# A prologue in a new order, stack loads in halves and last sums on three engines, in a fused attention and gMLP block

## The chip, the cores and the metric

The kernel runs on one core of one Trainium2 chip. The metric is device time of one execution in microseconds; shown are the median of three runs and one execution taken by the hardware profiler. The core has five engines that run side by side and wait for each other by semaphores: PE (TensorE, matrix products; PEld is its weight load), DVE (VectorE), ACT (ScalarE), POOL (GpSimd) and SP (SyncE, which here only issues DMAs). DMAs move data between the chip's main memory and the on-chip memory.

## What is computed

A transformer block with two parallel branches on one sequence of S = 2048 tokens of width D = 512, 32 heads of 16, and a hidden width of 1792, split in two halves of 896:

```python
xn = layernorm(x)
q, k, v = split_heads(xn @ wqkv)                 # 32 heads of 16
o = softmax(q @ k.T / 4) @ v                     # per head, 2048 x 2048 scores
attention = merge(o) @ wo
z = gelu(xn @ w_in)
z1, z2 = z[:, :896], layernorm(z[:, 896:])
g = w_sp @ z2 + b_sp[:, None]                    # mixes over the tokens
mlp = (z1 * g) @ w_out
out = x + attention + mlp
```

All is float32. Where a product needs more than the matmul's own precision, an operand is written as the sum of two parts ("split" into high and low), and three products are added.

## The kernel before

**One program in two pieces.** The instruction streams of all engines are written out in order by the kernel itself; nothing reorders them afterwards. The first piece, the *prologue*, is a list of words, `STEPS`, which the class `First` turns into instructions one word at a time, so the place of a word fixes the place of its instructions on every engine that it uses. The second piece comes from a *planner* in the kernel's host code: it keeps a planned clock for each engine, asks at each step what TensorE may do next and emits it.

**Words of the list.** The four groups g of 512 tokens are written as the first digit:

- S: statistics of two token tiles on VectorE (bn_stats, L1006); R: their reciprocal root; N: the normalisation on GpSimd (L1023), with a star the second tile on ACT.
- T: four transposes on TensorE (L1028) into a PSUM tile; E: copy of the result to SBUF, split, by ACT and VectorE (L244).
- Q g a: the projection to q (a = 0) or k (a = 1) of the first eight heads, 12 matmuls (L247 to L249). F g a: its eviction, split and store to main memory (`qscr`, `kscr`; two DMAs). Without a star ACT makes the high part and VectorE the low part (L244); with one ACT copies twice and GpSimd subtracts (L1058).
- L g: the load of the first head pair's q and k *stacks* for that token group back into SBUF (`qst`, `kst`; four DMAs of 96 KB). M kc t: a product of q tile t and k group kc (L1100, TensorE), for which the stacks must have landed; X kc t: its row maximum on VectorE (L1105).
- VH, VL: the split of the weight of v (a star: on GpSimd, L1076 and L1082); V, VE: the first tiles of v. WH, WL, B: split of the weights of q and k and of the bias. Z g c: a 512 KB store of the transposed tokens to `xscr`, by SP. The other twelve such stores (tokens of groups 1 to 3) are issued by GpSimd behind the list (`keep`, L1142).

A PSUM tile is taken in turn out of four, so a T, Q, V or M also waits until the tile's last reader is through.

**DMAs.** `move` (L142) issues on SP, in the order of the program. SP uses eight completion semaphores in turn, so each DMA waits until the one eight before it has landed.

**The planner.** The attention runs over 16 head pairs p, four groups of 512 queries c and 16 key tiles kt. TensorE's stream is made of *scores* (S, L1212), *maxima* of the pair to come (M, L1226; the maximum is L823 on VectorE), *value groups* (V, L1313: 32 matmuls on eight exponentials; 128 of them, V1 to V128) and *dense* slots (D, L1271), which take the rest of the block's products from a queue: rest of v, rest of q and k, z2, z1, the mixing over tokens (`spatial`, with pieces `zs0` to `zs111` of z2 and the split weight `wsp`), the gMLP's output product and at last the attention's output product (`attn_out`). A slot is two matmuls of 512 columns on the two halves of the array. `ORDER` is the pattern between two value groups. Where nothing else may be issued, the planner emits a *filler* slot (L1285), a product with zeros.

`LOADZ` is the planned time from the issue of a `zs` piece to its landing; the planner lets no dense slot that uses it stand earlier than that by its clock. `hold` (L1252) stops the queue at a unit's end in a gap between two value groups once more than eight dense slots have been placed in it.

**Stacks.** `load_stacks` (L802) loads the q and k stacks of pair p + 1 while pair p runs: four DMAs of 384 KB, spaced 2.7 us apart in the planner's clock (`later`, unit `HALF`).

**The end.** The last pair's heads go through `last_pair` (L943, sums of the softmax), `last_norm` (L955, reciprocal and product on VectorE), `last_mm` (L964, product with `wo`, by way of a selection) and `last_add` (L971), which adds the product to `fin`, the finished rest of two token tiles (t = 0, 2, ... 14), and stores it. `last_turn` decides when a `last_mm` may come. Tasks have a priority; a lower number goes first.

Of the kernel before, what the change touches and what calls it, by code (L numbers as in the profile page):

```python
# [16 lines left out]
P = 128  # L17
# [29 lines left out]
PF = 8  # L47
WARM = 22
STEPS = (
# [5 lines left out]
)  # L55
CYC = 8
FINE = 24
LOAD = 5.0
LOADZ = 5.0
HALF = 2.7  # L60
SLOT = 0.23
TURN = 0.2
# [6 lines left out]
def fused_block(ctx, tc, x, wqkv, wo, w_in, w_spT, b_sp, w_out, out):  # L69
# [18 lines left out]
    def ta(n):  # L88
        return 0.2 + n / 1220.0
# [51 lines left out]
    def move(dst, src):  # L141
        nc.sync.dma_start(raw(dst), raw(src))  # L142
# [13 lines left out]
    def later(k, fn, *args):  # L156
        at(clock() + k * HALF, fn, *args)
# [34 lines left out]
    def spawn(gen, prio=2, ready=None):  # L192
        count[0] += 1
        ends[0] = clock() if ready is None else ready
        queue_up(gen, prio, count[0], ends[0])
# [606 lines left out]
    def load_stacks(p, cols=slice(0, S)):  # L802
        m, r = p // 4, (p % 4) * 2
        q, k = qst[p % 2], kst[p % 2]
        sl = [slice((r + j) * DH, (r + j + 1) * DH) for j in range(2)]
        for j in range(2):
            for i, (t, scr) in enumerate(((q, qscr), (k, kscr))):
                args = t[64 * j:64 * j + KS, cols], scr[m][sl[j], :, cols]
                if p and 2 * j + i:
                    later(2 * j + i, move, *args)  # L810
                else:
                    move(*args)

    NSTEP = NP * 64
    mmax = {}
# [127 lines left out]
    def last_pair(c, e, k):  # L943

        ones = sel["ones"]
        two = piece(f"on{c}").bitcast(F32)
        rec, on = two[:, 0, 0:P], two[:, 1, 0:P]
        acc = sl[k][:, 1, :]
        for b in (1, 0):
            for u in range(4):  # L950
                nc.tensor.matmul(acc[32 * u:32 * u + 32, b * P:(b + 1) * P], ones[:, 0, 32 * b:32 * b + 32], e[:, u * P:(u + 1) * P], start=True, stop=True)
        T["P"] += 0.5
        spawn(last_norm(c, acc, rec, on, k), 0, T["P"] + 0.2)

    def last_norm(c, acc, rec, on, k):  # L955
        yield "D", 0.95
        nc.vector.reciprocal(rec, acc[:, P:2 * P])  # L957
        yield "D", 0.3
        nc.vector.tensor_mul(on, acc[:, 0:P], rec)
        free_slot(k)  # L960
        for i in range(2):
            turn.append((c, on, ends[0] + 0.1, i))
# [6 lines left out]
        spawn(last_add(4 * c + 2 * i, k), 0, T["P"] + 0.2)  # L969

    def last_add(t, k):  # L971
        yield "D", 1.22
        nc.vector.tensor_add(fin[t], sl[k], fin[t])
        free_slot(k)
        for a in range(2):
            after(0.1, move, out[(t + a) * P:(t + a + 1) * P, :], fin[t][:, a, :])

# [136 lines left out]
    with tc.manual_schedule(engines=engines):  # L1114
# [64 lines left out]
        def free_slot(k):  # L1179
            pending[k] -= 1  # L1180
            if not pending[k]:
                slotfree[k], kind[k] = ends[0] + 0.08, ""
# [54 lines left out]
        def has_dense(t):  # L1237
            nonlocal blocked, swap, hold, seen
            while not slots:
                if blocked > t or dfree[0] > t or hold or not queue:  # L1240
                    return False
                it = next(queue[0], None)
                if it is None:
                    queue.pop(0)
                elif it[0] == "t":
                    slots.extend(it[1])
                elif it[0] == "w":
                    blocked = t + it[1]
                elif it[0] == "s":
                    swap = True  # L1250
                elif it[0] == "q":
                    hold = spent > 8 and n_pv < N and len(vdone) == NT - EARLY  # L1252
                elif it[0] == "e":
                    dfree[0] = FAR
                    held[0] = len(it[1])
                    for g in it[1]:
                        spawn(g, 0, T["P"] + 0.25)
            if swap and seen < lastd:
                nc.tensor.drain()
                seen = pe  # L1260
                T["P"] += DRAIN
            swap = False
            return True
# [81 lines left out]
        def spare(t):  # L1345
            return [k for k in range(3) if slotfree[k] <= t]

        def last_turn(t):
            c, on, when, i = turn[0]
            if when > t or added.get(4 * c + 2 * i, FAR) + 0.1 > t or len(spare(t)) < 2:  # L1350
                return False
            turn_to("L")
            last_mm(c, on, i, take("l"))
            turn.pop(0)
            return True
# [77 lines left out]
```

## Time and profile before

| | |
|---|---|
| median of three runs | 1849.95 us (1849.7 to 1851.14) |
| profiled execution, its own time | 1848.92 us |
| its span in the profile | 1847.1 us |
| TensorE busy | 1809.0 us |
| VectorE busy | 1445.7 us |
| ScalarE busy | 1210.1 us |
| GpSimd busy | 673.9 us |
| row maxima on VectorE (L823) | 1008 of 1222 ns |
| exponentials on ScalarE (L86) | 1024 of 1026 ns |

In timelines a row is: start, length, engine, line, operation, destination and source, count, and in brackets the engine's idle time just before it and what ended it. In the chain of waits a row is start, length, and the engine or transfer that the end hung on. Windows give each engine's busy time in a stretch, the granted clock of TensorE as a share of full speed, the busy share of the DMA engines and their rate.

### The profile page before, as it was taken

To read this page: it belongs to the slowest core of one execution; us is meant where nothing else is said; L and a number is where in the kernel's file an instruction comes from. 1 tells how busy PE (TensorE), PEld (TensorE's weight loads), DVE (VectorE), ACT (ScalarE), POOL (GpSimd) and SP (SyncE) were. 2 spreads that over 40 slices of the span, in tenths; PEclk is the share of its full clock that TensorE was granted. 3 is DMA by queue.
4 is the path that set the end of the run, shared out by engine and by line. 5 is a ranking of instruction groups with operands and counts; after the bars stand their busy time and mean duration, and the time that the engine had idled before them with its cause. 6 is when DMAs were issued, how large, how long until landed. Compare 5 with 4: busy or idle time off the path is not lost.

```text
span 1847.1 us, 38060 instructions
## 1 busy us (share of the span) xinstructions
PE 1809.0 (98%) x14774; PEld 1094.1 (59%) x14774; DVE 1445.7 (78%) x1700; ACT 1210.1 (66%) x1329; POOL 673.9 (36%) x778
## 2 busy tenths in 40 slices
PE   8999999999999999999999999999999999999998
PEld 6655656656656656566665655656556566665543
DVE  7857887888887877778877887778778878787883
ACT  4247777888877777666666665666656666565665
POOL 3442142677758677112532244103422240002200
PEclk9999999999999999999999999999999999999999
DMA  7666754434664337657857567665767566575422
GB/s 273 236 235 197 218 193 147 122 110 121 162 201 118 123 82 217 151 150 180 220 160 202 155 193 186 163 148 158 181 170 183 178 177 141 143 185 141 128 86 81
DMA packets 211069, 305.63 MB, mean 165 GB/s; under 512 B 36784, under 2 KB 106992, under 8 KB 208000
## 3 DMA queue, kind: packets, MB, share of 16 engines
q1 hardware_dynamic: 203400, 275.93, 53.8%
q0 software_dynamic: 7488, 27.27, 4.3%
q8 instruction: 116, 1.90, 0.4%
q14 instruction: 65, 0.53, 0.1%
HBM read 193.27 MB, written 109.85 MB: 164 GB/s over the span
## 4 chain that ended last, share of the span: by engine, by line
PE 87%; DVE 5%; DMA 3%; POOL 1%; issue 1%; SPq 1%; ACT 1%; DVEq 0%; POOLq 0%; ACTq 0%
PE dps L1271 35%; PE sl L1313 23%; PE sl L1212 14%; PE sl L1226 12%; DVE mm L823 4%; SPq L142 1%; PE dps L1285 1%; DMA zs<-z2scr 1%; POOL wsp L288 1%; PE sl L247 1%; PE sl L249 0%; PE sl L248 0%; ACT pf L86 0%; DMA wsp_10r<-in_w_spT 0%; PE sl L967 0%
## 5 line engine op out<-in xcount | busy, mean ns | idle before, releaser
L823 DVE TENSOR_REDUCE mm<-sl 128x2 f32<-128x1024 f32 x1008 | 1208.0, 1222 | 200.5 <-PE sl L1226 193.0
L86 ACT ACTIVATE pf<-sl 128x1024 f32<-128x1024 f32 x1024 | 1042.5, 1026 | 327.4 <-PE sl L1212 288.5
L1313 PE MATMUL sl<-pf,vall 128*32 128x512 f32 x4096 | 467.9, 595 | 0.7 <-DVE on L957 0.6
L1212 PE MATMUL sl<-qst,kst 50*128 50x512 f32 x2048 | 434.8, 418 | 8.4 <-DVE mm L823 2.5
L1226 PE MATMUL sl<-kst,qst 48*128 48x512 f32 x2016 | 414.9, 404 | 4.5 <-DVE mm L823 2.9
L1271 PE MATMUL dps<-wsp,zs 64*128 64x512 f32 x2352 | 380.3, 393 | 2.2 <-DMA zs<-z2scr 1.8
L1212 PEld LDWEIGHTS sl<-qst,kst 50*128 50x128 f32 x2048 | 194.5, 184 | 220.8 <-issue 82.1
L1313 PEld LDWEIGHTS sl<-pf,vall 128*32 128x32 f32 x4096 | 119.3, 109 | 266.6 <-issue 234.6
L1226 PEld LDWEIGHTS sl<-kst,qst 48*128 48x128 f32 x2016 | 192.3, 185 | 101.9 <-ACT pf L86 49.5
L1271 PEld LDWEIGHTS dps<-wsp,zs 64*128 64x128 f32 x2352 | 227.5, 187 | 40.7 <-DMA zs<-z2scr 2.5
L86 ACT ACTIVATE e<-sl 128x512 f32<-128x512 f32 x64 | 38.3, 598 | 199.5 <-PE sl L1313 188.5
L1335 DVE TENSOR_TENSOR e<-sl,e 128x512 f32<-128x512 f32 x64 | 44.3, 692 | 119.3 <-PE sl L1313 53.6
L729 POOL TENSOR_TENSOR hhl<-z1i,hhl 128x512 fp32r<-128x512 f32 x28 | 36.0, 1292 | 271.7 <-ACT hhl L86 271.7
L1271 PE MATMUL dps<-w,xt 64*128 64x448 f32 x768 | 110.4, 368 | 1.7
L1271 PE MATMUL dps<-wout,hp 64*128 64x512 f32 x672 | 109.9, 392 | 0.0
L874 POOL TENSOR_TENSOR ob<-ob 128x512 f32<-128x512 f32 (+1 forms) x16 | 20.5, 1281 | 198.2 <-DMA ob<-rscr 181.5
L1271 PEld LDWEIGHTS dps<-w,xt 64*128 64x128 f32 x768 | 73.4, 186 | 16.4 <-issue 8.5
L1271 PEld LDWEIGHTS dps<-wout,hp 64*128 64x128 f32 x672 | 65.1, 187 | 9.4
L397 POOL TENSOR_TENSOR qkhl<-qr,qkhl 128x512 fp32r<-128x512 f32 x24 | 30.4, 1283 | 102.0 <-ACT qkhl L86 79.0
L1271 PE MATMUL dps<-wf,zs 64*128 64x512 f32 x336 | 55.3, 392 | 0.1
L870 POOL TENSOR_TENSOR ob<-ob 128x512 f32<-128x512 f32 (+1 forms) x16 | 20.9, 1306 | 93.2 <-DMA ob<-escr 90.9
L1271 PE MATMUL dps<-xnT,wqk 64*128 64x512 f32 x288 | 48.1, 394 | 0.3
(290 smaller groups left out, 1699.2 us busy)
## 6 DMA issues: line engine op xcount, KB each, us to landing
zs<-z2scr SPq DMA_DIRECT2D x192, 256.0 KB
escr<-e SPq DMA_DIRECT2D x60, 256.0 KB
hscr<-hhl POOLq DMA_DIRECT2D x28, 512.0 KB, 6.6
qst<-qscr SPq DMA_DIRECT2D x30, 384.0 KB
kst<-kscr SPq DMA_DIRECT2D x30, 384.0 KB
qscr<-qkhl SPq DMA_DIRECT2D x16, 512.0 KB
kscr<-qkhl SPq DMA_DIRECT2D x16, 512.0 KB
xt<-xscr SPq DMA_DIRECT2D x64, 128.0 KB
```

What stands on the lines that cost most here:

```text
L86: return nc.scalar.activation(out, in_, func, **kw)
L142: nc.sync.dma_start(raw(dst), raw(src))
L397: nc.gpsimd.tensor_sub(hl[:, 1, :], raw_, hl[:, 0, :].bitcast(F32))
L729: nc.gpsimd.tensor_sub(hl[:, 1, :], z1, hl[:, 0, :].bitcast(F32))
L823: nc.vector.tensor_reduce(mmax[g][:, :, t, kc], sl[k], AX.X, ALU.max)
L870: nc.gpsimd.tensor_add(both_[rows, 0, :], both_[rows, 0, :], both_[rows, 1, :])
L874: nc.gpsimd.tensor_mul(both_[rows, 0, :], both_[rows, 0, :], both_[rows, 1, :])
L1212: nc.tensor.matmul(sl[k][:, j, :], kst[p % 2][rows, kt * P:(kt + 1) * P], qst[p % 2][rows, c * 512:(c + 1) * 512], start=True, stop=True)
L1226: nc.tensor.matmul(sl[k][:, j, :], qst[p % 2][rows, tt * P:(tt + 1) * P], kst[p % 2][rows, kc * 512:(kc + 1) * 512], start=True, stop=True)
L1271: nc.tensor.matmul(dps[:, bank, :w], lhs, rhs, start=go, stop=stop)
L1313: nc.tensor.matmul(sl[k][cols:cols + VW, 0, :], vpack(kt + r, 2 * p + j), pf[:, j * 512:(j + 1) * 512], start=n % CYC == 0, stop=n % CYC = ...
L1335: nc.vector.tensor_add(e, sl[k][:, 0, :], e)
```

## The change

Six edits in one:

- `STEPS` is another list. The number of words of each kind is the same. The four Z words stand at its end. Z stores were on SP in the middle. One F more has a star (three instead of two), three VL instead of one, and two N instead of five; most other words stand in another order.
- `LOADZ` goes from 5.0 to 6.5.
- `load_stacks` of pairs from the second on is cut in two halves of the columns: eight DMAs of 192 KB, each half a unit after the one before.
- `last_norm` has priority -1 instead of 0.
- `last_add` of t = 8 and 10 copies the product to SBUF on ACT and adds on GpSimd (planned 2.6 us).
- `hold` depends on there being maxima left (`n_mx < NSTEP`), and `last_turn` needs one free PSUM tile instead of two once the values are done.

```diff
 STEPS = (
-    "S00 S01 R00 WH0 N00 WL0 R01 S10 N01* T01 S11 WH1 T03 E03 T00 E01 R10 T02 WL1 E02 E00 R11 N10 N11* Q00 T13 T12 "
...
-    "X01 M23 VE3 X22 V0 VE0 X12 M21 X23 M20 X21 L3 M11 V1 X20 M32 M30 X11 M31 X32 X31 VE1 V2 X30 M33 X33 VE2 "
+    "S00 S01 R00 WH0 N00 WL0 R01 N01 S10 S11 T01 T02 WH1 R10 E01 R11 T00 N11 T03 E02 WL1 N10 E00 VH2* E03 S21 VH3* "
...
+    "VE0 M20 L3 M23 X20 M22 X23 X22 V1 M33 M31 VE1 X33 M32 V2 M30 X32 X31 X30 VE2 Z00 Z01 Z02 Z03 "
 )
-LOADZ = 5.0
+LOADZ = 6.5
...
-        for j in range(2):
-            for i, (t, scr) in enumerate(((q, qscr), (k, kscr))):
-                args = t[64 * j:64 * j + KS, cols], scr[m][sl[j], :, cols]
-                if p and 2 * j + i:
-                    later(2 * j + i, move, *args)
-                else:
-                    move(*args)
+        n = 0
+        for part in (slice(0, S // 2), slice(S // 2, S)) if p else (cols,):
+            for j in range(2):
+                for t, scr in ((q, qscr), (k, kscr)):
+                    args = t[64 * j:64 * j + KS, part], scr[m][sl[j], :, part]
+                    if n:
+                        later(n / 2, move, *args)
+                    else:
+                        move(*args)
+                    n += p > 0
...
-        spawn(last_norm(c, acc, rec, on, k), 0, T["P"] + 0.2)
+        spawn(last_norm(c, acc, rec, on, k), -1, T["P"] + 0.2)
...
     def last_add(t, k):
-        yield "D", 1.22
-        nc.vector.tensor_add(fin[t], sl[k], fin[t])
-        free_slot(k)
+        if t // 4 == 2:
+            copy = piece(f"last{t}").bitcast(F32)
+            yield "A", ta(1024)
+            act(copy, sl[k], AF.Copy)
+            free_slot(k)
+            yield "G", 2.6
+            nc.gpsimd.tensor_add(fin[t], copy, fin[t])
+        else:
+            yield "D", 1.22
+            nc.vector.tensor_add(fin[t], sl[k], fin[t])
+            free_slot(k)
...
-                    hold = spent > 8 and n_pv < N and len(vdone) == NT - EARLY
+                    hold = spent > 8 and n_mx < NSTEP and len(vdone) == NT - EARLY
...
-            if when > t or added.get(4 * c + 2 * i, FAR) + 0.1 > t or len(spare(t)) < 2:
+            if when > t or added.get(4 * c + 2 * i, FAR) + 0.1 > t or len(spare(t)) < 1 + (n_pv < N):
```

What moves in the engines' order is shown at three places.

The first is SP's queue in the prologue, before, around the load of group 1's stacks, L1. Names end in the group and the number of the tile; `qscr0<-qkhl0_0_1` is the store of F10, and the four loads of `qst0` and `kst0` behind it are L1:

```order
L142 DMA kscr0_98<-qkhl0_1_1_509 128x2x512
L142 DMA kscr0_98<-qkhl0_1_1_509 128x512
L142 DMA xscr0_1_103<-xnT0_1_329 128x1024
L142 DMA qscr0_94<-qkhl0_0_1_532 128x2x512
L142 DMA qscr0_94<-qkhl0_0_1_532 128x512
L142 DMA qst0_90<-qscr0_94 48x512
L142 DMA kst0_92<-kscr0_98 48x512
L142 DMA qst0_90<-qscr0_94 48x512
L142 DMA kst0_92<-kscr0_98 48x512
L142 DMA qscr0_94<-qkhl0_0_2_604 128x2x512
L142 DMA qscr0_94<-qkhl0_0_2_604 128x512
```

And now, where `qkhl0_0_2` is F20's store and the four `xscr` stores are the Z words behind the last load, L3:

```order
L142 DMA qscr0_94<-qkhl0_0_1_553 128x2x512
L142 DMA qscr0_94<-qkhl0_0_1_553 128x512
L142 DMA qscr0_94<-qkhl0_0_2_575 128x2x512
L142 DMA qscr0_94<-qkhl0_0_2_575 128x512
L142 DMA qst0_90<-qscr0_94 48x512
L142 DMA kst0_92<-kscr0_98 48x512
L142 DMA qst0_90<-qscr0_94 48x512
L142 DMA kst0_92<-kscr0_98 48x512
L142 DMA kscr0_98<-qkhl0_1_2_618 128x2x512
L142 DMA kscr0_98<-qkhl0_1_2_618 128x512
```

```order
L142 DMA qscr0_94<-qkhl0_0_3_683 128x512
L142 DMA qst0_90<-qscr0_94 48x512
L142 DMA kst0_92<-kscr0_98 48x512
L142 DMA qst0_90<-qscr0_94 48x512
L142 DMA kst0_92<-kscr0_98 48x512
L142 DMA xscr0_0_102<-xnT0_0_349 128x1024
L142 DMA xscr0_1_103<-xnT0_1_326 128x1024
L142 DMA xscr0_2_104<-xnT0_2_343 128x1024
L142 DMA xscr0_3_105<-xnT0_3_353 128x1024
L142 DMA wqk1_0r_767<-in_wqkv 128x4x128
```

Ahead of L1 the store of a token tile is gone and F20's store has come; the Zs follow L3.

The second is SP's queue in the mixing stage, where the stacks of pair 10 (`qst0`, `kst0`) are loaded between the pieces `zs60` and `zs61`; `os` and `ob` are loads for the attention's normalisation, `mscr` row maxima. Before:

```order
L142 DMA qst0_90<-qscr2_96 48x2048
L142 DMA wsp2_14r_12561<-in_w_spT 128x512
L142 DMA kst0_92<-kscr2_100 48x2048
L142 DMA wsp2_15r_12595<-in_w_spT 128x512
L142 DMA qst1_91<-mscr2_165 2x16x32 x2
L142 DMA qst0_90<-qscr2_96 48x2048
L142 DMA zs60_12642<-z2scr_118 64x2x512 x2
L142 DMA kst0_92<-kscr2_100 48x2048
L142 DMA os1_3_12546<-escr1_3_138 128x1x32 x2
L142 DMA ob1_3_12547<-escr1_3_138 128x1x512 x2
L142 DMA zs61_12674<-z2scr_118 64x2x512 x2
L142 DMA escr2_1_140<-e9_1_12540 128x512
```

And now:

```order
L142 DMA kst0_92<-kscr2_100 48x1024
L142 DMA qst1_91<-mscr2_165 2x16x32 x2
L142 DMA qst0_90<-qscr2_96 48x1024
L142 DMA kst0_92<-kscr2_100 48x1024
L142 DMA zs60_12683<-z2scr_118 64x2x512 x2
L142 DMA qst0_90<-qscr2_96 48x1024
L142 DMA os1_3_12584<-escr1_3_138 128x1x32 x2
L142 DMA ob1_3_12585<-escr1_3_138 128x1x512 x2
L142 DMA zs61_12715<-z2scr_118 64x2x512 x2
L142 DMA kst0_92<-kscr2_100 48x1024
L142 DMA escr2_1_140<-e9_1_12578 128x512
```

Between `zs60` and `zs61` stood a whole `kst0`; now half a `qst0` stands there, and the last half of `kst0` comes behind `zs61`.

The third is TensorE at the program's end: L967 (now L970) is `last_mm`, L951 (now L954) `last_pair`, L1285 (now L1296) fillers, L1271 (now L1282) dense slots. Before:

```order
L1313 MATMUL sl0_201<-pf1022_19982,vall_87 32x512 x2
L1313 MATMUL sl0_201<-pf1023_19990,vall_87 32x512 x2
L1285 MATMUL dps_200<-brow_85,zeror_81 128x512 x2
L967 MATMUL sl1_202<-sel_18192,on1_19768 128x512 x2
L967 MATMUL sl2_203<-sel_18192,on2_19892 128x512 x2
L951 MATMUL sl0_201<-e15_3_19942,sel_18192 32x128 x8
L1285 MATMUL dps_200<-brow_85,zeror_81 128x512 x8
L967 MATMUL sl1_202<-sel_18192,on2_19892 128x512 x2
L1285 MATMUL dps_200<-brow_85,zeror_81 128x512 x2
L967 MATMUL sl2_203<-sel_18192,on3_20013 128x512 x2
L1285 MATMUL dps_200<-brow_85,zeror_81 128x512 x2
L967 MATMUL sl0_201<-sel_18192,on3_20013 128x512 x2
```

And now:

```order
L1324 MATMUL sl2_203<-pf1023_20014,vall_87 32x512 x2
L970 MATMUL sl0_201<-sel_18347,on1_19773 128x512 x2
L970 MATMUL sl1_202<-sel_18347,on2_19910 128x512 x2
L1282 MATMUL dps_200<-wo1_18433,op14_1_19794 128x512 x2
L970 MATMUL sl2_203<-sel_18347,on2_19910 128x512 x2
L1282 MATMUL dps_200<-wo2_18449,op14_1_19794 128x512 x2
L954 MATMUL sl0_201<-e15_3_19960,sel_18347 32x128 x8
L1282 MATMUL dps_200<-wo2_18449,op14_1_19794 128x512 x4
L1282 MATMUL dps_200<-wo3_18463,ohl3_3_19478 128x512 x6
L970 MATMUL sl1_202<-sel_18347,on3_20049 128x512 x2
L970 MATMUL sl2_203<-sel_18347,on3_20049 128x512 x2
L1296 MATMUL dps_200<-brow_85,zeror_81 128x512 x10
```

Dense slots of `attn_out` for the last two token tiles (`op14`, with `wo`) stand where fillers stood, five of them between the last softmax sums and the products of the last group; the two products of the group before stand ahead of the sums.

Over the whole program TensorE's rows differ by 30 filler matmuls, 150 in place of 180. From the end of the prologue to V88 every engine but SP has the same order as before.

6 rows, old and new, of the table STEPS are left out of this document.

## The prediction

> **What bounds the kernel now.** I read the page first (busy times, costliest groups), then the windows by stage, then the order of TensorE's, VectorE's and the DMA queue's work in the windows where TensorE falls short of full, and the chain of waits there. From the page:
>
> ```profile
> span 1847.1 us, 38060 instructions
> PE 1809.0 (98%) x14774; PEld 1094.1 (59%) x14774; DVE 1445.7 (78%) x1700; ACT 1210.1 (66%) x1329; POOL 673.9 (36%) x778
> L823 DVE TENSOR_REDUCE mm<-sl 128x2 f32<-128x1024 f32 x1008 | 1208.0, 1222 | 200.5 <-PE sl L1226 193.0
> L86 ACT ACTIVATE pf<-sl 128x1024 f32<-128x1024 f32 x1024 | 1042.5, 1026 | 327.4 <-PE sl L1212 288.5
> L729 POOL TENSOR_TENSOR hhl<-z1i,hhl 128x512 fp32r<-128x512 f32 x28 | 36.0, 1292 | 271.7 <-ACT hhl L86 271.7
> ```
>
> TensorE is the bound: 38.1 us of the span are not busy. Time can come only from those, from matmuls left out, or from a faster granted clock. Windows (columns: length, busy time of PE, PEld, DVE, ACT, POOL, then granted clock, DMA share, GB/s) say where it falls short:
>
> ```profile
> 30.00:40.00 10.00, 9.99 (x54) 7.69 (x53) 8.28 (x13) 4.88 (x10) 0.00 (x0) 1.00 1.00 365
> 40.00:50.00 10.00, 6.65 (x20) 4.41 (x19) 4.49 (x5) 0.60 (x1) 0.00 (x0) 0.75 0.60 214
> 50.00:60.00 10.00, 10.00 (x46) 6.76 (x44) 6.50 (x7) 1.69 (x3) 0.00 (x0) 0.91 0.68 251
> 60.00:70.00 10.00, 9.43 (x52) 6.43 (x50) 9.20 (x13) 1.31 (x3) 4.03 (x6) 1.00 0.50 154
> 1100.00:1150.00 50.00, 48.11 (x386) 29.18 (x388) 36.35 (x41) 29.62 (x30) 28.45 (x30) 0.97 0.86 215
> 1337.60:1351.30 13.70, 13.70 (x119) 8.62 (x117) 10.06 (x14) 8.27 (x9) 1.30 (x1) 1.00 0.54 128
> 1351.30:1366.90 15.60, 15.20 (x125) 8.84 (x123) 12.18 (x15) 8.60 (x9) 2.69 (x3) 1.00 0.58 165
> 1555.60:1717.10 161.50, 160.13 (x1348) 97.66 (x1350) 130.07 (x143) 101.48 (x102) 12.88 (x16) 1.00 0.59 150
> 1717.10:1799.10 82.00, 78.89 (x619) 42.50 (x620) 69.46 (x79) 49.31 (x50) 14.86 (x14) 1.00 0.34 104
> 1834.40:1847.10 12.70, 8.80 (x58) 3.69 (x58) 8.38 (x9) 0.00 (x0) 0.00 (x0) 1.00 0.67 250
> ```
>
> So: the prologue between 40 and 60, one place near 1144, and the end. From 1150 on TensorE is nearly full, so there only matmuls left out count. The prologue, TensorE (matmuls in pairs or threes, start, length) and then VectorE:
>
> ```profile
> 44.16 0.47 PE L1100 MATMUL sl<-kst,qst 48*128 48x512 f32 x1 [2.46 <-DMA kst<-kscr]
> 45.52 1.22 PE L1100 MATMUL sl<-kst,qst 48*128 48x512 f32 x3 [0.89 <-DMA kst<-kscr]
> ...
> 47.69 0.63 PE L249 MATMUL dps<-xnT,wqk 128*128 128x512 f32 x1
> 48.12 0.63 PE L247 MATMUL dps<-xnT,wqk 128*128 128x512 f32 x1
> ...
> 53.20 0.39 PE L249 MATMUL sl<-qst,xnT 128*128 128x512 f32 x1
> 53.43 0.40 PE L247 MATMUL sl<-kst,xnT 128*128 128x512 f32 x1
> ```
>
> ```profile
> 36.35 0.68 DVE L1082 TENSOR_TENSOR kst<-wv2r,kst 128x512 fp32r<-128x512 f32 x1
> ...
> 46.35 1.23 DVE L1105 TENSOR_REDUCE mm<-sl 128x2 f32<-128x1024 f32 x1 [4.81 <-PE sl L1100]
> ...
> 52.51 1.23 DVE L1105 TENSOR_REDUCE mm<-sl 128x2 f32<-128x1024 f32 x1 [3.21 <-PE sl L1100]
> ...
> 67.62 1.23 DVE L1105 TENSOR_REDUCE mm<-dps 128x2 f32<-128x1024 f32 x1 [0.32 <-PE dps L1100]
> ```
>
> Maxima M13 and M10 wait for group 1's stacks (L1): 2.46 and 0.89 us idle. Then matmuls start 0.43 us apart instead of 0.23 (47.69 to 48.12 against 53.20 to 53.43): half speed for the 12 of Q30. VectorE, which owes sixteen maxima of 1.23, idles 4.81 and 3.21. Why L1 is late, from the DMA queue and the chain:
>
> ```profile
> 33.96 0.95 SPq L142 DMA_DIRECT2D xscr<-xnT  x1
> 35.01 2.24 SPq L142 DMA_DIRECT2D qscr<-qkhl  x2
> 41.17 0.32 SPq L142 DMA_DIRECT2D qst<-qscr  x1
> ```
>
> ```profile
> 36.00 5.11 DMA qscr<-qkhl
> 42.66 2.82 DMA kst<-kscr
> ```
>
> F10's store lands at 41.11, only then can the queue load L1, whose last part lands at 45.48.
>
> **The prologue.** Three token stores of 512 KB (Z03, Z02, Z01) leave SP's queue ahead of L1, Z00 ahead of L3; all four now stand behind L3. Their 512 KB each at the window's 365 GB/s is 1.4 us of transfer. In the new order of SP, L1 stands behind F11's and F20's stores instead; F11* and F20* are split by ACT and GpSimd, and one fewer F plus two fewer VL run on VectorE.
>
> I walked both lists with the rows' durations (0.23 a matmul, 0.68 a split, 1.23 a maximum, 2.8 a load's latency). In the new one L1 lands at 40.5, or 41.9 with GpSimd's own 512 KB store in front, and M13 wants it at 43.5: both waits go. So 2.46 + 0.89 = 3.35, and the slow clock 12 x (0.43 - 0.23) = 2.4. VectorE carries three splits fewer, 3 x 0.6 from start to start = 1.8 us, in a list that ends with its last maximum; earlier first maxima spare 0.3 of its idle time. Sum 7.85. What is late next: L2 lands at 45.8 to 47.3 for a matmul at 47.3, and L3 at 53.7 to 54.7 for one at 54.7. I take 0.35 for these, **7.5** in all. Bounds: 8.4 if nothing is late, 3 if L2 is 1 us late and the clock falls again (1 + 2.4 + 1 for L3). GpSimd's six operations more (three of them splits, 1.3 each by the page) end before M13; they put F20's store where the walk has it. The Zs land before the row maxima are stored; the next reader, a later stage, is far behind.
>
> The Trainium skill, "TensorE: Matmul & The Clock Gate", section "What's actually happening", has the clock halve only after an idle window of about 3.4 us. The halving agrees with 0.43 against 0.23; the longest single idle here is 2.46, so this trace shows it with less. By that rule a short wait would cost only itself and the 2.4 above would have another cause: that is a rival below.
>
> **The stack loads in halves.** From group 1 on each load is eight DMAs instead of four: 60 more issues of 0.3 to 0.6 on SP, the same bytes. A DMA also waits for the landing of the eighth one before it, so a spatial piece (zs, two DMAs) can be held by halves. At 1127 this is what it looks like now:
>
> ```profile
> 1128.87 0.58 SPq L142 DMA_DIRECT2D kst<-kscr  x1
> ...
> 1132.12 1.82 SPq L142 DMA_DIRECT2D zs<-z2scr  x2
> ```
>
> ```profile
> 1133.34 10.89 DMA zs<-z2scr
> ```
>
> ```profile
> 1143.35 0.50 PE L1271 MATMUL dps<-wsp,zs 64*128 64x512 f32 x1 [1.34 <-DMA zs<-z2scr]
> 1144.27 1.22 PE L1271 MATMUL dps<-wsp,zs 64*128 64x512 f32 x3 [0.42 <-DMA zs<-z2scr]
> ```
>
> A whole kst (384 KB) lies between pieces zs60 and zs61, zs61 takes 10.89 us to land, TensorE waits 1.34 + 0.42 and the clock falls: the 50 us window lost 1.9 idle and 0.03 x 50 = 1.5 by the clock, 3.4 in all. After the change half a qst lies there and the last half kst comes behind zs61. At that window's 215 GB/s 192 KB fewer are 0.9 us. I take the waits of 1.76 as shortened by 1.0, the rest too short to slow the clock: gain 1.0 + 1.5 = **2.5**, between 3.4 and, if zs61 is held by a landing instead, 0; a loss is the last rival. The maxima of the next stacks lie many microseconds behind their loads, so the later last half costs them nothing.
>
> **The dense order from V88 on.** Planned landings of z pieces go from 5.0 to 6.5 us, and the hold for the last product stays on until the maxima end. TensorE's rows fall only by 30 filler matmuls (180 to 150), two to a slot. Counting slots by value group, V89 to V117 lose 25 (24 dense ones, moved to the end, and a filler; V90 falls from 27 dense to 11 with 7 fillers). A slot costs, eight matmuls being four slots:
>
> ```profile
> 1153.55 1.09 PE L1271 MATMUL dps<-wsp,zs 64*128 64x512 f32 x8
> 1154.47 0.41 PE L1212 MATMUL sl<-qst,kst 50*128 50x512 f32 x2
> ```
>
> From 1153.55 to the next at 1154.47 is 0.92 / 4 = 0.23, so 25 x 0.23 = 5.8. Windows of V91 and V92 (1337.6 to 1366.9) and of V106 to V117 (1555.6 to 1717.1) are PE-full. But the window 1717.1 to 1799.1, six groups with only 18 dense slots, has TensorE 3.1 us short and VectorE at 69.46 of 82: below some 35 slots a group goes no faster, 13.7 us each. V90 at 35 slots touches that. I take **5.4**; bounds 3 (only V91 to V93 and V102 pay) and 7 (V92's 0.4 of idle goes as well). V118 takes six of the slots with its VectorE-bound time as cover; V119 to V124 stay.
>
> **The tail.** The dense slots that were held come back in V127 and V128 in place of fillers, so their cover is the exponentials that ACT paces there; two or three slots more than fillers before, 0 to 0.7. Behind the last value group VectorE had six sums of 1.22 and a normalisation; now four of its own, one dense eviction more late, and t = 8 and t = 10 by an ACT copy (1.03, the page's row of 1024 columns) and a GpSimd sum of about 2.6 (twice the page's 1.292 for 512 columns). The last sum before is this:
>
> ```profile
> 1842.26 1.22 DVE L973 TENSOR_TENSOR fin<-sl,fin 128x1024 f32<-128x1024 f32 x1 [0.27 <-PE sl L967]
> ```
>
> By this the two end 5.9 and 8.5 us after the last value matmul, the last VectorE sum at 9.45 against 9.1 before; the output store follows as now. Together **+0.6** (from -0.3 to +1.5): with priority -1 the last normalisation no longer waits behind sums, but five dense slots stand ahead of its products.
>
> **Sum.** 1848.92 (the profiled execution, 1.8 above its span) - 7.5 - 2.5 - 5.4 + 0.6 = 1834.1. The median of the runs shown, 1849.95, is 1.0 above that execution, so about 1835.
>
> **Rivals.**
> *Late stacks.* L2 or L3 misses its matmul by over a microsecond, and the clock falls as at 46.67. For it speak margins of 0 to 1 us; against it the 4.2 us of queue freed by moving three Zs. Prologue gain 3: 1839.5.
> *The clock is not tied to these waits.* Then 2.4 in the prologue and 1.5 at 1144 stay: 1835 + 3.9 = 1839. Against it speaks that the two slow stretches of those windows start right behind the waits. This is what the Trainium skill's clock page would give.
> *The halves do nothing.* zs61 waits for its eighth predecessor, the stall of V76 stays: 1837.5. This is also the case "the change does not do what it says".
> *Halves fill the queue (slower).* Fifteen loads of eight DMAs, in a queue where each DMA waits for the eighth before it. If zs or weight pieces behind them come late, each such place costs what V76 does, 3.4. The gains of 14.8 are eaten by 4.4 places, and slower by over 0.2% (3.7 us, about what a measurement here can tell from no change) needs 18.5 / 3.4, six of the fifteen loads; at seven it is 1835 + 24 = 1859. Against it: same bytes, and only one load of fifteen stalls TensorE now. The Trainium skill, "DMA: Bandwidth & Descriptors", sections "Anatomy of one DMA" and "Rules for kernel authors", prices a DMA at about 2.0 us fixed and advises coalescing. By it four more would add 8 us to a load if nothing overlapped. Here L1's four, issued 41.17 to 42.66, were all landed at 45.48, so they overlap.
>
> **Chances.** Forecast 0.60 (own range 1831 to 1838), late stacks 0.14, clock 0.04, halves do nothing 0.12, queue filled 0.10. The first four are all faster, 0.90; of the last I count 0.03 within 0.2% and 0.07 slower. Low end: all gains at their bounds, 8.4 + 3.4 + 7 + 0.3 = 19.1, gives 1831; I go to 1830. High end: late stacks with the dense term at 3 and the tail at +1.5 is 1835 + 4.5 + 2.4 + 0.9 = 1843.
>
> **What would show it.** Right: the list's last maximum ends near 61 instead of 68.85; TensorE never waits over 1 us for kst there and the clock stays full from 40 to 60; between 1140 and 1148, some 8 us earlier in time, TensorE idles less than 0.8 us; V90 near 13.6; the end 12.7 to 14 us behind the last value matmul. Wrong: a wait on zs, wsp or kst of over 1 us at a place that has none now, or groups V91 to V117 that keep their time with fewer slots.

## The result and the profile after

The changed kernel takes 1838.58 us (median of 4 runs, 1837.59 to 1839.77) against 1849.83 (4 runs, 1848.6 to 1851.14): a ratio of 0.994, 95% interval 0.9925 to 0.9955, 11.3 us less. Forecast were 1835, 14.8 less, and a range from 1830 to 1843. The profiled execution took 1837.59 with a span of 1835.7, so spans can be compared: 11.4 us less.

From the page of the changed kernel:

```profile
span 1835.7 us, 38100 instructions
PE 1800.9 (98%) x14744; PEld 1087.7 (59%) x14744; DVE 1443.6 (79%) x1695; ACT 1211.2 (66%) x1329; POOL 684.3 (37%) x786
```

TensorE is busy 8.1 us less and idle 3.3 less. Where this lies is read from the starts of the value groups in the two traces (V0 is the first one issued, V125 the last whole one, all in us from the span's start):

| stretch | before | after | difference | forecast |
|---|---|---|---|---|
| start to V0 | 94.29 | 86.86 | -7.43 | -7.5 |
| V0 to V75 | 1036.67 | 1037.09 | +0.42 | 0 |
| V75 to V76 | 18.45 | 16.63 | -1.82 | -2.5 |
| V76 to V88 | 160.80 | 160.84 | +0.04 | 0 |
| V88 to V118 | 406.85 | 401.78 | -5.07 | -5.4 |
| V118 to V125 | 90.96 | 90.87 | -0.09 | 0 |
| V125 to the last value matmul | 26.38 | 26.93 | +0.55 | } +0.6 |
| last value matmul to the end | 12.75 | 14.71 | +1.96 | } |

Windows of the changed kernel (columns as before), with the prologue, the place of V76's stall, V92 (1351.3 to 1366.9 before), and the twelve groups that stood at 1555.6 to 1717.1 before (V107 to V118 by this count; the prediction calls them V106 to V117):

```profile
10.00:20.00 10.00, 8.83 (x42) 7.31 (x43) 9.62 (x27) 4.80 (x11) 7.09 (x10) 0.83 0.87 319
...
40.00:50.00 10.00, 10.00 (x47) 6.74 (x46) 8.01 (x9) 1.79 (x3) 0.00 (x0) 1.00 0.82 280
50.00:60.00 10.00, 10.00 (x49) 6.94 (x49) 9.11 (x8) 1.47 (x3) 0.00 (x0) 1.00 0.75 269
...
1100.00:1150.00 50.00, 48.48 (x402) 29.34 (x396) 37.41 (x43) 30.45 (x32) 23.36 (x25) 1.00 0.80 197
```

```profile
1340.80:1354.50 13.70, 13.70 (x120) 8.03 (x119) 11.18 (x12) 9.18 (x9) 1.29 (x1) 1.00 0.40 117
1543.40:1703.20 159.80, 159.80 (x1346) 95.67 (x1344) 130.49 (x143) 101.18 (x102) 12.87 (x16) 1.00 0.60 154
```

TensorE is full from 40 to 60 and its clock too, where it had 6.65 of 10 and 0.75. VectorE's last maximum of the list, and TensorE's two waits for zs61:

```profile
60.16 1.23 DVE L1116 TENSOR_REDUCE mm<-dps 128x2 f32<-128x1024 f32 x1 [0.33 <-PE dps L1111]
```

```profile
1135.68 0.50 PE L1282 MATMUL dps<-wsp,zs 64*128 64x512 f32 x1 [0.68 <-DMA zs<-z2scr]
1136.89 0.72 PE L1282 MATMUL dps<-wsp,zs 64*128 64x512 f32 x3 [0.71 <-DMA zs<-z2scr]
```

The last maximum ends at 61.39 instead of 68.85. The waits for zs61 went from 1.34 and 0.42 to 0.68 and 0.71; they shrank by 0.4 only, but the clock held, and that is most of the 1.8. The end, VectorE and GpSimd first and then the stores on SP:

```profile
1827.83 2.36 DVE L984 TENSOR_TENSOR fin<-sl,fin 128x1024 f32<-128x1024 f32 x2 [0.17 <-PE sl L970]
```

```profile
1823.75 4.72 POOL L981 TENSOR_TENSOR fin<-last,fin 128x1024 f32<-128x1024 f32 x2 [63.44 <-issue]
```

```profile
1829.09 0.81 SPq L142 DMA_DIRECT2D out<-fin  x2
1829.99 0.89 SPq L142 DMA_DIRECT2D out<-fin  x2
1830.98 1.19 SPq L142 DMA_DIRECT2D out<-fin  x2
```

VectorE's last sum ends at 1830.19, 9.2 behind the last value matmul, as forecast (9.45; before it was 9.1). But the end comes 5.5 us after that sum, where before it came 3.6 after it (1843.48 to 1847.1): the stores of t = 12, 10 and 14 now stand one behind the other. While they flow the DMA engines are full (share 1.03, 382 GB/s):

```profile
1830.01:1834.01 4.00, 0.00 (x0) 0.00 (x0) 0.18 (x1) 0.00 (x0) 0.00 (x0) 0.74 1.03 382
```

The last three pairs of stores before, for comparison; the second row holds two pairs, the last of which starts at 1843.51:

```profile
1840.69 0.81 SPq L142 DMA_DIRECT2D out<-fin  x2
```

```profile
1842.02 2.33 SPq L142 DMA_DIRECT2D out<-fin  x4
```

### The profile page after: what moved, and what is told of

Same layout as the page of the kernel before. It is cut to its first block, busy times and chain, and to the rows that moved or that the text cites. A ratio compares the mean times of both kernels' runs of the same rounds, so it can differ in the third digit from the quotient of the medians.

```text
span 1835.7 us, 38100 instructions
## 1 busy us (share of the span) xinstructions
PE 1800.9 (98%) x14744; PEld 1087.7 (59%) x14744; DVE 1443.6 (79%) x1695; ACT 1211.2 (66%) x1329; POOL 684.3 (37%) x786
## 4 chain that ended last, share of the span: by engine, by line
PE 91%; DVE 4%; DMA 2%; issue 1%; ACT 1%; SPq 1%; POOL 0%; DVEq 0%; POOLq 0%; ACTq 0%
PE dps L1282 36%; PE sl L1324 24%; PE sl L1223 14%; PE sl L1237 12%; DVE mm L826 4%; PE dps L1296 1%; SPq L142 1%; PE sl L247 1%; DMA zs<-z2scr 1%; PE sl L248 1%; PE sl L249 1%; ACT pf L86 0%; PE sl L970 0%; DMA wsp_14r<-in_w_spT 0%; PE sl L1039 0%
## 5 line engine op out<-in xcount | busy, mean ns | idle before, releaser
L1282 PE MATMUL dps<-wsp,zs 64*128 64x512 f32 x2352 | 381.0, 392 | 2.2 <-DMA zs<-z2scr 1.4
L1282 PEld LDWEIGHTS dps<-wsp,zs 64*128 64x128 f32 x2352 | 227.6, 187 | 38.5 <-DMA zs<-z2scr 2.1
L1282 PE MATMUL dps<-w,xt 64*128 64x448 f32 x768 | 110.5, 368 | 1.7
L1282 PE MATMUL dps<-wout,hp 64*128 64x512 f32 x672 | 110.5, 392 | 0.1
L1282 PEld LDWEIGHTS dps<-w,xt 64*128 64x128 f32 x768 | 73.7, 186 | 16.1 <-issue 8.5
L1282 PEld LDWEIGHTS dps<-wout,hp 64*128 64x128 f32 x672 | 64.3, 187 | 10.2 <-issue 0.5
L1282 PE MATMUL dps<-wf,zs 64*128 64x512 f32 x336 | 55.6, 393 | 0.1
L1282 PE MATMUL dps<-xnT,wqk 64*128 64x512 f32 x288 | 48.0, 394 | 0.3
```

The costliest lines, as they stand in the source:

```text
L1282: nc.tensor.matmul(dps[:, bank, :w], lhs, rhs, start=go, stop=stop)
```

## The experiments

Each experiment is one profiled execution; the last three kernels were also timed five or six times. Numbers without a count of runs are from the one profiled execution. Where the instructions are the same as in the changed kernel up to some place, the runs also show how much that place varies.

### The prologue: the list, its Z words, the clock

**The old list in the changed kernel.**

```diff
 STEPS = (
-    "S00 S01 R00 WH0 N00 WL0 R01 N01 S10 S11 T01 T02 WH1 R10 E01 R11 T00 N11 T03 E02 WL1 N10 E00 VH2* E03 S21 VH3* "
...
-    "VE0 M20 L3 M23 X20 M22 X23 X22 V1 M33 M31 VE1 X33 M32 V2 M30 X32 X31 X30 VE2 Z00 Z01 Z02 Z03 "
+    "S00 S01 R00 WH0 N00 WL0 R01 S10 N01* T01 S11 WH1 T03 E03 T00 E01 R10 T02 WL1 E02 E00 R11 N10 N11* Q00 T13 T12 "
...
+    "X01 M23 VE3 X22 V0 VE0 X12 M21 X23 M20 X21 L3 M11 V1 X20 M32 M30 X11 M31 X32 X31 VE1 V2 X30 M33 X33 VE2 "
```

> The changed kernel with the list of before; all else as changed. Theory (the list alone makes the prologue's 7.4 us): the last maximum of the list ends at 68.8 again, TensorE waits 2.5 and 0.9 for kst, the span is 1835.7 + 7.4 = 1843.1. Rival (part of it comes from the other edits, such as the Zs' place relative to later loads): the first value group starts before 93, the span is below 1841.

Span 1843.6, 7.9 more. V0 starts at 95.23, the last maximum ends at 69.79. TensorE's rows there:

```profile
45.04 0.47 PE L1111 MATMUL sl<-kst,qst 48*128 48x512 f32 x1 [2.51 <-DMA kst<-kscr]
46.45 1.22 PE L1111 MATMUL sl<-kst,qst 48*128 48x512 f32 x3 [0.94 <-DMA kst<-kscr]
```

The waits of the kernel before are back to a tenth of a microsecond; all else of the table stays. The prologue's gain is the list's. (V0 is 0.9 later than in the kernel before. M13 already is 0.9 later here, at 45.04 instead of 44.16, and the clock from 10 to 20 is 0.83 here and was 1.00 there.)

**The new list with the Z words back in front of the loads.**

```diff
-... E11 L0 E10 ... Q21 L1 M01 ... VE0 M20 L3 ... VE2 Z00 Z01 Z02 Z03
+... E11 Z03 Z02 L0 E10 ... Q21 Z01 L1 M01 ... VE0 M20 Z00 L3 ... VE2
```

> The new list with the four Z words put back in front of the loads: Z03 and Z02 before L0, Z01 before L1, Z00 before L3, as they stood before. Theory (the token stores ahead of the loads make them late, and a late load halves the clock): TensorE waits over 1 us for kst at M13 or later, matmuls 0.43 apart follow, and 3 to 6 of the 7.4 us are lost, span 1838.7 to 1841.7. Rival (the order of the words and the work taken off VectorE make the gain, the Zs fit beside): less than 1.5 lost, span below 1837.2.

Span 1842.8: 7.1 lost, more than the theory's 6. V0 starts at 94.22. Not L1 but group 3's stacks (L3, behind Z00) are the latest:

```profile
58.72 0.46 PE L1112 MATMUL dps<-kst,qst 48*128 48x512 f32 x1 [1.11 <-DMA kst<-kscr]
60.07 0.77 PE L1112 MATMUL dps<-kst,qst 48*128 48x512 f32 x1 [0.89 <-DMA kst<-kscr]
...
62.22 0.63 PE L249 MATMUL sl<-kst,xnT 128*128 128x512 f32 x1
62.65 0.63 PE L250 MATMUL sl<-kst,xnT 128*128 128x512 f32 x1
```

```profile
60.00:70.00 10.00, 9.36 (x35) 6.31 (x37) 5.82 (x10) 0.60 (x1) 5.21 (x7) 0.66 0.40 141
```

Two waits of 2.0 us together, then matmuls 0.43 apart and a granted clock of 0.66 (a wait of 0.69 for kst at 50.10 comes before them). With the token stores in the middle the new order is worth nothing, V0 at 94.22 against 94.29 before; the rival is out.

**The old list with only its Z words moved to the end.**

```diff
-... B VH0 Z03 N30* ... T23 Z02 L0 F11 Z01 E23 ... M22 M12 Z00 X01 ... VE2
+... B VH0 N30* ... T23 L0 F11 E23 ... M22 M12 X01 ... VE2 Z00 Z01 Z02 Z03
```

> The list of before with only its four Z words moved to the end; all else as changed. Theory (the Zs are the cause of the late L1): the waits of 2.46 and 0.89 for kst shrink to under 1 together, the clock stays full, 3.5 to 5.8 of the 7.4 us are won, span 1837.3 to 1839.6. Rival (order and engines make the gain): the waits stay over 2 us, under 2 us won, span over 1841.

Span 1836.5, V0 at 89.06, only 2.20 later than with the new list. L1 is in time; what remains are two waits for group 3:

```profile
57.04 0.47 PE L1112 MATMUL dps<-kst,qst 48*128 48x512 f32 x1 [0.36 <-DMA kst<-kscr]
57.99 0.50 PE L1112 MATMUL dps<-kst,qst 48*128 48x512 f32 x1 [0.48 <-DMA kst<-kscr]
```

So of the 7.4 us the four Z words alone make 5.2, and the other 129 words with the work taken off VectorE make another 2.2. The two don't simply add: with the Zs in the middle the same 129 words were worth 0.1. The span is only 0.8 longer, since V47 happened to be 0.8 shorter in this run.

**More warming matmuls.**

```diff
-WARM = 22
+WARM = 30
```

> The changed kernel with 30 instead of 22 warming matmuls at the start, which end at about 11 to 12 instead of 9.07. In the changed kernel the granted clock falls to 0.66 and 0.50 between 12 and 16, behind 1.8 us of idle in four pieces below 0.5 us each. Theory (the clock follows the busy share of the last few microseconds, not one long idle): the clock stays at 1.00 from 12 to 16, Q00's matmuls are 0.23 apart, and 0.5 to 1.1 us are won, span 1834.6 to 1835.2. Rival (VectorE, 9.6 of 10 us busy there, sets the pace): the clock stays full but under 0.3 us is won; or the clock falls all the same.

The clock is 1.00 from 10 to 20 instead of 0.83, and V0 starts at 87.22, 0.36 later. Span 1835.5, nothing won: the rival holds, VectorE (9.62 of 10 busy in both) sets the pace there. In the changed kernel idle pieces below 0.5 us each were followed by a lower clock; that cost nothing here.

### The stacks

**Whole loads again.**

```diff
-        n = 0
-        for part in (slice(0, S // 2), slice(S // 2, S)) if p else (cols,):
-            for j in range(2):
...
+        for j in range(2):
+            for i, (t, scr) in enumerate(((q, qscr), (k, kscr))):
+                args = t[64 * j:64 * j + KS, cols], scr[m][sl[j], :, cols]
+                if p and 2 * j + i:
+                    later(2 * j + i, move, *args)
+                else:
+                    move(*args)
```

> The changed kernel with the stack loads whole again (four DMAs of 384 KB); the order of all engines but SP is the same. Theory (the halves shortened the stall of V76): V76 takes 18.4 instead of 16.6, TensorE waits 1.3 and 0.4 for zs61, the clock falls behind it, span 1837.5. Rival (halves fill the queue elsewhere as much as they spare here, V47's 0.7 among it): V76 longer, others shorter, span within 0.5 of 1835.7. Third (the stall is V76's phase against the shorter prologue, not the halves): V76 stays 16.6.

V76 takes 20.58, TensorE waits for zs61:

```profile
1138.54 0.50 PE L1279 MATMUL dps<-wsp,zs 64*128 64x512 f32 x1 [2.39 <-DMA zs<-z2scr]
1140.09 0.73 PE L1279 MATMUL dps<-wsp,zs 64*128 64x512 f32 x3 [1.05 <-DMA zs<-z2scr]
```

Span 1840.7, 5.0 more, 4.0 of it here. The direction is the theory's, the size twice as large. One execution doesn't give it well: with halves and the same order at this place, V76 took 16.1 to 18.8 in ten profiled kernels (mean 17.0), with whole loads 18.45 and 20.58. The means lie 2.5 apart, but two of the ten with halves are above the 18.45, so with only two executions of whole loads the size of the gain stays open. No other stretch is shorter with whole loads by more than 0.3, so this run shows no queue filled by the halves elsewhere.

### The dense order

**The planned landing back at 5.0.**

```diff
-LOADZ = 6.5
+LOADZ = 5.0
```

> The changed kernel with LOADZ = 5.0. By the order of TensorE this puts V89 to V118 back to the slots of before (1177.5 instead of 1152.5 between V89 and V117) and leaves V127 and V128 to fillers. Theory (5.2 us there are the 25 slots): V88 to V118 take 5.0 to 5.3 longer, the last value matmul comes 0.5 less than that later, span 1839.5 to 1841. Rival (the stretch gains by the earlier clock of the DMAs, not by slots): under 2 longer, span under 1837.7.

V88 to V118 takes 407.42 instead of 401.78, 5.6 more and a little over the 5.0 to 5.3 expected, and the values end 0.6 sooner after V125; span 1841.6. Theory. So the one number, not `hold`, makes the whole gain of that stretch. V0 was late by 1.2 in this run. Behind the last value matmul fillers stand here where the changed kernel has dense slots, and yet the end comes 14.66 after it: those dense slots are not what makes the end late.

### The end

**The sums of t = 8 and 10 on VectorE.**

```diff
-        if t // 4 == 2:
-            copy = piece(f"last{t}").bitcast(F32)
-            yield "A", ta(1024)
...
-            nc.gpsimd.tensor_add(fin[t], copy, fin[t])
-        else:
...
+        yield "D", 1.22
+        nc.vector.tensor_add(fin[t], sl[k], fin[t])
+        free_slot(k)
```

> The changed kernel with the sums of t = 8 and 10 on VectorE again; the rest of the end as changed. By the profile of the changed kernel the VectorE chain grows by two sums of 1.22, less what it idles before the last reciprocal (1.75): last sum some 0.7 to 1.3 later than 9.17 us behind the last value matmul. Theory (the end's 1.9 us come from the six last stores standing in one queue behind GpSimd's late sum): the stores go out one pair at a time again, 3.6 us from last sum to end as before, end 13.5 to 14.1 behind the last value matmul instead of 14.7, span 1834.6 to 1835.1. Rival (the stores are late for another reason, as the dense slots there): 5.5 us from last sum to end stay, span 1836.4 to 1837.

The last sum ends 10.66 us behind the last value matmul, 1.5 later than in the changed kernel, and the end comes 4.2 after it instead of 5.5: 14.82 in all, where 13.5 to 14.1 was expected. Both halves of the theory come, the first larger and the second smaller than expected, and they cancel. In six kernels with the same instructions at the end as the changed kernel it came at 14.44 to 14.73, so the 0.1 us that the two sums on GpSimd bring is no gain that can be told from none. (The span, 1841.6, is longer for other reasons: V0, V47 and V76 were 1.3, 2.5 and 2.1 late.)

**The old condition of hold.**

```diff
-                    hold = spent > 8 and n_mx < NSTEP and len(vdone) == NT - EARLY
+                    hold = spent > 8 and n_pv < N and len(vdone) == NT - EARLY
```

> The changed kernel with the old condition of hold (until the values end). By the order only V127 and V128 differ: nine dense slots and a filler in V127 instead of eleven, nine instead of seven behind the last value group. Theory (dense slots between the paced exponentials cost 0.5, and the end is set by VectorE and the stores): span within 0.4 of 1835.7. Rival (the slots behind the last value group set the end): two more cost 0.5 to 0.9.

The end takes 16.39: t = 14's eviction comes behind t = 12's sum, the last sum ends at 10.73. The rival, and more than it said: with two more slots the last sum is 1.5 later and the end 1.7, while the values end 0.3 sooner. The new condition is worth some 1.3 at the end.

**Stores on two queues.**

```diff
+    def put(dst, src):
+        nc.scalar.dma_start(raw(dst), raw(src))
...
-            after(0.1, move, out[(t + a) * P:(t + a + 1) * P, :], fin[t][:, a, :])
+            after(0.1, put if t // 4 == 2 else move, out[(t + a) * P:(t + a + 1) * P, :], fin[t][:, a, :])
```

> The changed kernel with the last stores of t = 8 and 10 issued by ACT instead of SP. Theory (the end's loss is the six last stores on one queue behind GpSimd's late sum): t = 10's pair goes out at 8.9 behind the last value matmul beside that of t = 12, t = 14's at 9.3 instead of 10.0, and the end comes 0.7 to 1.4 earlier: 13.3 to 14.0 instead of 14.7. Rival (the transfers themselves set the end, whoever issues them): 14.4 or later.

End at 14.56. The pair of t = 10 goes out at 7.46 behind the last value matmul instead of 8.98, and that of t = 14 at 9.21 instead of 9.96, for a gain of 0.15 us, which is within the spread of the end. The rival: a second queue brings nothing that can be measured.

**GpSimd's sums at t = 4 and 6, the last softmax sums first.**

```diff
-        if t // 4 == 2:
+        if t // 4 == 1:
...
-            if turn and (n_st - n_pv < 2 or n_st == N) and last_turn(t):
-                continue
             if n_pv == N and sel and urgent and urgent[0][2] <= t and free:
                 turn_to("V")
                 last_pair(*urgent.pop(0)[:2], take("o"))
                 continue
+            if turn and (n_st - n_pv < 2 or n_st == N) and last_turn(t):
+                continue
```

> The changed kernel with GpSimd's two sums at t = 4 and 6 instead of 8 and 10, and the last softmax sums ahead of waiting products. GpSimd's sums are then over near 5 us behind the last value matmul, VectorE's last near 8.2, and the stores go out pair by pair. Theory: last sum to end 3.6 to 4.2 again, end 11.8 to 12.6 behind the last value matmul instead of 14.7; 2.1 to 2.9 us faster than the changed kernel, beside a spread of some 2 from elsewhere. Rival (dense slots of t = 14 set the last sum): last sum at 9 or later, end 12.8 to 13.5.

1838.94 us (5 runs), ratio to before 0.9946, interval 0.9932 to 0.9959: no better. VectorE's last two sums start 6.1 behind the last value matmul and end 8.4 behind it, as the theory had it, and yet the end is at 14.73:

```profile
1828.92 2.35 DVE L984 TENSOR_TENSOR fin<-sl,fin 128x1024 f32<-128x1024 f32 x2
```

```profile
1825.45 8.37 SPq L142 DMA_DIRECT2D out<-fin  x12
```

The first of the twelve stores goes out at 2.6 (the value matmuls end at 1822.83) instead of 0.4, since t = 4 now waits for GpSimd and t = 8 comes first; from then on SP issues without a break, and the last lands at 13.56. But the line is not fed all that time. One issue takes 1.96 us, and from 5 to 6 us behind the last value matmul the DMA engines are nearly idle (share 0.09); only from 6 on are they full:

```profile
1827.83:1828.83 1.00, 1.00 (x8) 0.22 (x8) 1.00 (x1) 0.00 (x0) 0.00 (x0) 1.00 0.09 25
```

Why that issue took so long was not tried.

**The same with stacks loaded four scores earlier.**

```diff
-LATE = 24
+LATE = 20
```

> The same with the stack loads four scores earlier (LATE = 20), so that at V76 six of the eight halves go out ahead of the row maxima's store, on which SP stands idle, and none between zs60 and zs61. Theory (zs61 is late by what is queued ahead of it): the waits of 0.7 and 0.7 for zs61 go, V76 takes 14.5 to 15.3 instead of 16.6, 1.3 to 2 us faster than the kernel with the better end alone. Rival (what bounds zs61 is GpSimd's split of the weights, whose loads the halves now delay): V76 at 16 or more, no gain.

V76 takes 15.40, with one wait of 0.40 for zs61; 1838.75 us (5 runs), ratio 0.9946, interval 0.9933 to 0.9958. At this place the theory, but no measurable gain: other pieces vary by as much.

**The changed kernel with the last softmax sums first and LATE = 20.**

```diff
-LATE = 24
+LATE = 20
...
-            if turn and (n_st - n_pv < 2 or n_st == N) and last_turn(t):
-                continue
             if n_pv == N and sel and urgent and urgent[0][2] <= t and free:
...
+            if turn and (n_st - n_pv < 2 or n_st == N) and last_turn(t):
+                continue
```

> The changed kernel with the last softmax sums ahead of waiting products (sums of t = 8 and 10 on GpSimd as changed) and LATE = 20. The stores of t = 4 and 6 leave early as in the changed kernel (0.4 and 2.4 us behind the last value matmul), t = 12 before t = 10. Theory (what the end costs is how late the first stores go and how many stand together at its end): last sum near 8.2, only t = 14's pair behind it, end 12.6 to 13.6 behind the last value matmul instead of 14.7; with V76 at 15.4 as in the run before, 1 to 3 us faster than the changed kernel. Rival (twelve stores of 256 KB need their time whatever the order): end at 14 or later, no gain beyond V76's 1.2.

End at 13.78, 0.9 sooner, with the last sum at 9.5 (8.2 was expected) and only t = 14's pair behind it. The line of the last six starts at 7.1 behind the last value matmul instead of 8.1:

```profile
1829.17 1.81 SPq L142 DMA_DIRECT2D out<-fin  x4
```

```profile
1831.63 0.83 SPq L142 DMA_DIRECT2D out<-fin  x2
```

So both theory and rival had a part. V76's stall moved: V75 takes 15.02 instead of 13.0, with a wait of 1.02 for a `wsp` split of GpSimd; that the halves now ahead of its loads are the reason is argued, not shown. The clock falls behind this wait, and V76 itself takes 16.51, not 15.4:

```profile
1124.61 0.51 PE L1282 MATMUL dps<-wsp,zs 64*128 64x512 f32 x2 [1.02 <-POOL wsp L286]
1125.05 1.89 PE L1324 MATMUL sl<-pf,vall 128*32 128x512 f32 x8
```

1838.33 us (6 runs, 1836.16 to 1841.02), ratio 0.994, interval 0.9923 to 0.9957: not to be told from the changed kernel. None of the versions tried is measurably better than it.

## Why the prediction was right, and where it was not

**Prologue, forecast -7.5, measured -7.43.** The mechanism holds in each part: with the Zs in front a load is late and the clock halves (the new list with Z in the middle), with only the Zs moved 5.2 are won, and 2.2 more come from the rest once the Zs are out of the way, for which the walk had 1.8 + 0.3. The 5.2 stand against 5.75 for the two waits and the slow clock. But 0.84 of waits for group 3 were left, so the waits shrank by 2.5, and the other 2.7 are the clock's, where 2.4 was taken: the prediction counted the 12 matmuls of Q30, and the stretch at half speed in the kernel before is longer. By this row it lost up to 3.1 (half of 6.25), an estimate:

```profile
44.94:51.77 6.83, 6.25 (x15) 4.30 (x15) 2.95 (x3) 0.00 (x0) 0.00 (x0) 0.50 0.67 246
```

What was called late next is what came: in five of the ten profiled kernels with the new list and the Zs last, TensorE waits 0.5 to 0.9 for group 3, and V0 starts at 87.8 to 88.4; in the other five at 86.6 to 87.2. The clock never fell behind those waits. So the rival *late stacks*, with a wait of over 1 us and a slow clock, came in none of the ten, but half of them lose 1.3 us by a milder form of it, where the prediction took 0.35. That the profiled execution of the changed kernel is one of the other five, and meets the forecast to 0.1, is in part luck.

**Halves, forecast -2.5, measured -1.8.** The waits shrank by 0.4, not by 1.0, so the sign of under 0.8 us of idle there was missed (1.39); the 1.5 of slow clock went. Even that hangs on the execution: in two kernels with halves the waits for zs61 came to 2.0 and 2.1 and the clock fell all the same (0.91 from 1130 to 1150). Undone, V76 is 4 us longer in one execution; by the means of ten and two executions 2.5. Of the rival *queue filled* nothing showed: with whole loads no other stretch is shorter by more than 0.3. (The fixed 2.0 us for a DMA that the prediction quotes from the Trainium skill, "DMA: Bandwidth & Descriptors", section "Anatomy of one DMA", is stated there for DMAs that GpSimd issues; the stack loads are SP's.)

**Dense order, forecast -5.4, measured -5.07**, and 5.6 when LOADZ is put back. The count of slots holds by blocks: V89 to V93 lose 17 slots and 3.9 us, 0.23 each, V106 to V117 six slots and 1.1 us, and the six slots more in V118 cost nothing. Single groups are less even: V90 loses nine slots and 1.03 us, V92 three and 1.90 (its 0.4 us of idle went too).

**V0 to V75, forecast 0, measured +0.42.** This is V47's +0.73 less small gains. V47 takes 12.5 to 16.3 in kernels with the same order there; in the longest it waits 1.69 and 0.62 for GpSimd's split of weights. With whole loads it took 13.60 against 13.76, so the halves are not seen in it. Why it varies so was not tried.

**The end, forecast +0.6, measured +2.5.** This is the step that failed: "the output store follows as now". The last sum was placed well (9.45 forecast, 9.2 measured), and the 0.55 ahead of it lies in the stated 0 to 0.7. But three pairs of stores become ready within 1.8 us (GpSimd's sum of t = 10 ends at 1828.47, VectorE's of 12 and 14 at 1829.06 and 1830.19), so 1.5 MB stand in one line. From the first issue at 1829.09 to the landing of the last at 1834.57 are 5.5 us for six stores; 4.1 of them are transfer at full DMA engines (382 GB/s, 0.69 us for 256 KB), the rest is the start of the first and the landing of the last. Before, the last three pairs became ready within 2.8 us and went out at 1840.69, 1842.02 and 1843.51, and the line hardly grew. I had carried over the 3.6 us from last sum to end, though the change altered how many stores come together at the end. What shows the transfers as the bound is that the DMA engines are full almost to the last landing, that a second queue gains no more than 0.15, and that the end comes 0.9 sooner where the line of the last six starts 1.0 sooner (the last experiment). The sign of an end 12.7 to 14 us behind the last value matmul was missed with 14.71.

Together: the forecast sum was -14.8 and the spans differ by 11.4. Of the 3.4 between, the end makes 1.9, V76 0.7, V0 to V75 0.4, the dense order 0.3 and the prologue 0.1.

## What to carry to other kernels

Put stores that nobody reads soon behind the loads that somebody waits for, in the queue that issues both: four such stores cost 5 us here, about half of it by the clock that a late load takes down. At a program's end count the stores that become ready together, not only the last sum: taking two sums off VectorE was worth 0.1 us here at most, because the transfers then stood in line. Feed that line early and without a gap. And know how much a stall varies from one execution to the next before a term is credited to an edit.

## What the runs showed of the hardware

The clock falls with less than one long idle. Waits of 2.5 and 0.9, of 2.4 and 1.05, of 1.34 and 0.42, and of 1.11 and 0.89 us within some 3 us were followed by matmuls at half speed; 0.68 and 0.71, and 0.36 and 0.48, were not. The sum of the waits does not decide it: a single wait of 1.02 at V75 (the last experiment) and waits of 0.52 and 0.63 at V47 (stores on two queues) were followed by half speed too. In between it depends on the execution: at V76 waits of 1.24 and 0.80 left the window 1130 to 1150 at a granted clock of 1.00 in one kernel (the old condition of hold), while 2.0 in two waits brought it to 0.91 in another (the sums on VectorE). Behind a wait, the stretches at half speed lasted 3.41 us or twice that: 44.94 to 51.77 and 1144.03 to 1147.44 in the kernel before, 60.12 to 66.94 in the new list with the Zs in front, 1125.15 to 1128.57 in the last experiment. The Trainium skill's page "TensorE: Matmul & The Clock Gate", section "What's actually happening", has a free-running window of about 3.4 us, and the clock halved after an idle one. The lengths of the stretches and the two outcomes at V76 agree with a free-running window; that the whole window must be idle does not fit these runs.

At the start too it depends on the execution. With the same instructions the clock was 1.00 from 10 to 20 in the kernel before and 0.83 with its list in the changed kernel. With eight more warming matmuls it was 1.00, and nothing was won; but it was 1.00 from 8 to 16 in some kernels without them too (the old condition of hold for one).

Stores of 256 KB to main memory flow at 382 GB/s when they stand in a line (1830.01 to 1834.01, DMA share 1.03), which is 0.69 us each. A line of six took 5.5 us from its first issue to its last landing, 1.4 us more than that. With two of the six issued by ACT the end came 0.15 us sooner, within the spread of 14.44 to 14.73.
